# Attention with two feed-forward layers: the conversion steps of three weight blocks and four weight pieces at other turns of the attention loop

## The chip, the cores and the metric

One Trainium2 chip, one of its cores. The metric is device time in microseconds (us) of one execution, of which the median over the runs is taken; less is better. The engines are TensorE (PE, its weight loads PEld), VectorE (DVE), ScalarE (ACT), GpSimd (POOL) and SyncE (SP), which issues the DMAs here.

## What is computed

```python
# attention: q, k, v (2, 8, 768, 64); centroids (8, 16, 64)
q_assign = argmax(einsum('bhsd,hcd->bhsc', q_n, c_n)); k_assign likewise
mask = q_assign[:, :, :, None] == k_assign[:, :, None, :]
scores = where(mask, q @ k.T / sqrt(64), -1e9)
attn = softmax(scores)            # over keys
x = attn @ v                      # -> (1536, 512)
# first feed-forward layer: w_in (512, 2048), w_out (2048, 512), given as float64
x = (relu(x @ w_in) ** 2) @ w_out
# second: four experts, w1 (4, 512, 1024), w2 (4, 1024, 512)
out = sum_e p[:, e:e+1] * (relu(x @ w1[e]) @ w2[e])
```

## The kernel before

Every matrix product is made of several passes in fp32r: a tensor is split into a rounded part (`hi`) and what is left (`lo`).

**The attention loop.** There are 16 heads (batch times heads) of six query tiles of 128 rows, 96 tiles in all, and the loop `for g in range(NU)` makes one turn for each. Two heads form a pair, so a pair is 12 turns. Turn g does the following, on these engines:
- PE: the scores `s` of tile g+2 (L643), the transposes `t` of tile g in two halves (L676), a half of the product with the values (`po`, L690 and L692), and, in some turns, extra work in the two slots X1 and X2: transposes of the next pair's q and k (L388), its centroid scores (L469, turns 1 and 2 of a pair), their transposes (L485, turns 2 and 3) and those of the one-hot rows (L542, turn 7).
- DVE: the maximum `nb` of tile g+2 (L652) and the low halves `ptl` of tile g (L682), one behind each half's transposes; in some turns reductions of the assignment: `A` (L490, turns 2 and 3), `mx` (L526 in turn 4, L530 in turn 5).
- ACT: the exponential of tile g+1 (L663), the high halves `pth` (L681), and copies.
- POOL: the assignment's operations on `A` (L515 to L517 behind the first `mx`, L520 to L523 behind the second), splits of q, k and v, and the norm of the pair before.

The scores and the transposes have two PSUM buffers each. The transposes of tile g, half 0, use the buffer that `ptl` of tile g-1, half 0, has read; so they wait for that `ptl`, and the same holds for half 1.

**Order.** Within a turn the instructions are issued in an order written out by hand (`ORDER`, one list for even and one for odd turns; the engines run each its own part of it in order). DVE's part of an even turn is: M (the maximum of tile g+2), C, L0 and L1 (`ptl`), C, K, Y2; of an odd turn: M, C, L0, C, L1, Y2, K, C. C takes a queued step of the assignment, Y2 ends the work of slot X2 (its evacuation, `A` here), and K is the conversion slot: `convert()` issues what `convs` holds for this turn. R issues what `early` holds (loads, stacks, norm steps).

**Conversion.** The first layer's weights come as float64 words. `split64` (L145) makes a block of 512 columns into hi and lo in six steps: f1, f2, f4 (`tensor_scalar`, L161, L164, L167), f5, f6 (`scalar_tensor_tensor`, L172, L177), all on DVE on the one buffer `cva`, and f3, which is a cast on ACT (L182) and a subtraction on POOL (L186). There are four blocks of `w_in`'s first chunk, j = 0 to 3. Their steps are spread over the turns by `AT["conv"]` for j = 0, and for j = 1, 2, 3 over turns b0, b0+1, b0+2, b0+3, b0+4 and b0+9 with b0 = 30, 42, 54, which are turns 6 to 10 and 3 of a pair. The blocks are used at the end of the loop and behind it (`early_gemm1`).

**Pieces.** `load_piece` (L102) loads a quarter of half a chunk of the second matrix `w_out` (256 KB). Its eight DMAs go out in turns 46, 58, 70 and 82, two in each. They are converted behind the loop (`run_second`, `first_chunk`), the second half (pieces 4 to 7) by the third and fourth conversion there. Their buffer is that from which blocks 2 and 3 were read.

Of the kernel before, what the change touches and what calls it, by code (L numbers as in the profile page):

```python
# [26 lines left out]
WARM = [11, 3, 2, 6, 2, 3]  # L27
START = {'t': [0, 0, 1, 1], 'a': [3, 3, 4, 4, 7], 'stack1': 4, 'stack': 5, 'head': 2}
AT = {"stack1": (-11, -10), "stack": (-9, -9), "ohd": -7, "splitv": -3, "load": -10,
      "t": [-14, -13, -12, -11], "a": [-11, -10, -10, -9, -5], "conv": (8, 9, 10, 20, 21, 27), "pieces": 46,  # L30
      "norm": (11, 12, 16, 18, 19, 26), "in": (22, 34)}


# [1 line left out]
def moe_attention_kernel(  # L35
# [23 lines left out]
    NTT = S // 128  # L59
# [42 lines left out]
    def load_piece(half, n):  # L102

        if n == 0:
            raw_t[0, 1, half] = rawp.tile([128, 2048], F32, tag="raw", name="raw")
        r = raw_t[0, 1, half].bitcast(I32).rearrange("p (k f) -> p k f", k=2)
        kk, fs = n // 2, slice((n % 2) * 512, (n % 2) * 512 + 512)
        nc.sync.dma_start(out=r[:, kk, fs], in_=wo32[:, half * 2 + kk, fs])
# [36 lines left out]
    def split64(ci, part, j, cv, eng=None):  # L145

        jj = j % 2
        shp = [128, 512] if part else [128, 4, 128]

        def word(x):  # L150
            r = raw_t[ci, part, j // 2].bitcast(I32)
            if part == 0:
                r = r.rearrange("p (k f w) -> p k f w", k=4, w=2)
                return r[:, :, jj * 128:(jj + 1) * 128, x]
            return r.rearrange("p (k f w) -> p k f w", k=2, w=2)[:, jj, :, x]
        st = a_t[ci, part, j] = {}

        def f1():
            a = st["a"] = cv(shp)
            st["i"] = a.bitcast(I32)  # L160
            nc.vector.tensor_scalar(st["i"], word(1), 0x7FFFFFFF, None, op0=ALU.bitwise_and)  # L161

        def f2():
            nc.vector.tensor_scalar(st["a"], st["a"], 2.0 ** -15, None, op0=ALU.max)  # L164

        def f4():
            nc.vector.tensor_scalar(  # L167
                st["i"], st["i"], 3, 0x3FFFFFF8,
                op0=ALU.logical_shift_left, op1=ALU.bitwise_and)

        def f5():
            nc.vector.scalar_tensor_tensor(  # L172
                out=st["i"], in0=word(1), scalar=-0x40000000, in1=st["i"],
                op0=ALU.bitwise_and, op1=ALU.bitwise_or)

        def f6():
            nc.vector.scalar_tensor_tensor(  # L177
                out=st["i"], in0=word(0), scalar=29, in1=st["i"],
                op0=ALU.logical_shift_right, op1=ALU.bitwise_or)

        def f3h():
            nc.scalar.copy(w_block(part, j)[0], st["a"])  # L182

        def f3l():
            hi, lo = w_block(part, j)
            (eng or nc.gpsimd).tensor_tensor(lo, st["a"], hi.bitcast(F32), op=ALU.subtract)  # L186

        def f3():
            f3h()
            f3l()  # L190
        return [[f1, f2, f4, f5, f6], [f3], [f3h, f3l]]
# [20 lines left out]
    with tc.manual_schedule():  # L212
# [940 lines left out]
        def at(d, g, f):  # L1153
            d.setdefault(max(g, 0), []).append(f)
# [11 lines left out]
        for j in range(1, NH // 2):  # L1166
# [3 lines left out]
            for n, f in enumerate([pair_scores(j, 0), pair_scores(j, 1), pair_turn(j, 0),  # L1170
                                   pair_turn(j, 1), pair_hot(j)]):
                u = START["a"][n] if j == 1 else u0 + AT["a"][n]
# [8 lines left out]
        convs = {}  # L1181
        for j in range(NF):
            steps = [f for fs in split64(0, 0, j, cv_p[0])[0:2] for f in fs]
            b0 = (2 * j + 3) * NTT
            turns = AT["conv"] if j == 0 else [b0 + x for x in (0, 1, 2, 3, 4, 9)]
            for u, f in zip(turns, steps):
                at(convs, u, f)
        for n in range(8):
            at(convs, AT["pieces"] + n // 2 * 2 * NTT, lambda n=n: load_piece(n // 4, n % 4))
        for hp in range(NH // 2 - 1):  # L1190
            norm_steps(hp)

# [420 lines left out]
```

## Time and profile before

| | us |
|---|---|
| median of 3 runs | 1020.67 (1020.12 to 1021.22) |
| profiled execution | 1024.25 |
| its span, first to last instruction | 1022.5 |

| engine | busy us | share of the span |
|---|---|---|
| PE | 1007.5 | 99% |
| PEld | 895.3 | 88% |
| DVE | 730.6 | 71% |
| ACT | 556.3 | 54% |
| POOL | 611.9 | 60% |

The attention loop takes the stretch from about 19 to 252 us; the rest is the two layers. A row of groups reads: line, engine, operation, output<-inputs, shapes, count | busy us, mean ns of one | idle time of the engine before them, and what ended most of it. A row of a timeline reads: start, duration, engine, line, operation, count, and in brackets the idle time before it and who ended it. The first maximum that opens turn g is that of tile g+2.

### The profile page before, as it was taken

Reading aid. Unit: us, or ns where it says so; the run is one execution under the profiler, and the core shown is the slowest. Engines: PE = TensorE matmul, PEld = TensorE weight load, DVE = VectorE, ACT = ScalarE, POOL = GpSimd, SP = SyncE. Lnnn points to the kernel's source line nnn. Section 1 sums busy time; section 2 is a strip of 40 time slices with the busy share of each in tenths; the row PEclk is TensorE's granted clock in tenths of the full one; section 3 lists DMA queues with packets and bytes.
Section 4 is the critical chain, followed back from the end, with each engine's and each line's share of the span. In section 5 each row is a group of like instructions: output and inputs, shape, how many; then the busy total and the mean of one; then the engine's idle time right before and its main releaser. Section 6 shows DMA issues by size and latency. Waiting matters only on the chain.

```text
span 1022.5 us, 15046 instructions
## 1 busy us (share of the span) xinstructions
PE 1007.5 (99%) x5457; PEld 895.3 (88%) x5457; DVE 730.6 (71%) x1114; ACT 556.3 (54%) x1131; POOL 611.9 (60%) x630
## 2 busy tenths in 40 slices
PE   8999999999999999999999999999999999999998
PEld 7999999999888787888889889898888888898987
DVE  6889989888899987797586555567676555555554
ACT  5888888988655644456453443434443434433341
POOL 4577777773326654346586665766866756657550
PEclk8999999999999999999999999999999999999999
DMA  7468877853112212211012212222124122121101
GB/s 183 100 157 195 186 165 166 184 138 83 41 42 83 83 42 83 82 58 67 21 42 83 79 46 83 63 62 83 43 92 134 42 83 71 54 83 62 63 21 62
DMA packets 74067, 89.66 MB, mean 88 GB/s; under 512 B 27316, under 2 KB 50248, under 8 KB 73992
## 3 DMA queue, kind: packets, MB, share of 16 engines
q1 hardware_dynamic: 73992, 88.69, 31.8%
q8 instruction: 43, 0.70, 0.3%
q14 instruction: 32, 0.26, 0.1%
HBM read 62.58 MB, written 3.19 MB: 64 GB/s over the span
## 4 chain that ended last, share of the span: by engine, by line
PE 76%; DVE 18%; ACT 3%; issue 1%; POOL 1%; DMA 0%; DVEq 0%; POOLq 0%; ACTq 0%
PE bank L876 26%; PE bank L1038 26%; PE bank L904 7%; PE t L676 4%; PE s L643 4%; DVE ptl L682 3%; DVE nb L652 2%; PE po L690 2%; PE po L692 2%; PE bank L854 2%; DVE x L910 1%; PE m L469 1%; DVE cva L172 1%; DVE cva L167 1%; DVE cva L177 1%
## 5 line engine op out<-in xcount | busy, mean ns | idle before, releaser
L1048 DVE SCALAR_TENSOR_TENSOR x<-bank,pe_p,x 128x512 f32<-128x512 f32 x180 | 134.9, 750 | 182.8 <-PE bank L1038 182.7
L979 POOL TENSOR_TENSOR wxl<-raw,wxh 128x512 fp32r<-128x512 f32 x64 | 74.5, 1187 | 144.7 <-ACT wxh L978 144.7
L1038 PE MATMUL bank<-wzh,gb 128*128 128x512 f32 x384 | 135.4, 393 | 0.0
L1038 PE MATMUL bank<-wzh,ga 128*128 128x512 f32 x384 | 134.5, 393 | 0.0
L682 DVE TENSOR_TENSOR ptl<-t,pth 128x384 fp32r<-128x384 f32 x192 | 98.0, 549 | 18.0 <-ACT pth L681 17.4
L1007 ACT COPY fa<-bank 128x384 f32<-128x384 f32 x96 | 45.6, 475 | 117.8 <-PE bank L876 117.7
L876 PE MATMUL bank<-xa,wxh 128*128 128x384 f32 (+1 forms) x392 | 103.7, 345 | 0.0
L652 DVE TENSOR_REDUCE nb<-s 128x1 f32<-128x768 f32 x96 | 90.9, 946 | 11.5 <-PE s L643 10.8
L876 PE MATMUL bank<-xa,wyh 128*128 128x384 f32 (+1 forms) x344 | 89.3, 340 | 0.8 <-DVE fa L891 0.6
L663 ACT ACTIVATE p<-s,nb 128x768 f32<-128x768 f32 x96 | 88.0, 917 | 2.9 <-DVE nb L652 2.6
L681 ACT CAST pth<-t 128x384 fp32r<-128x384 f32 x192 | 84.0, 487 | 9.0 <-PE t L676 8.3
L676 PE MATMUL t<-identf,p 128*128 128x128 f32 x576 | 85.8, 276 | 1.6 <-DVE ptl L682 1.4
L643 PE MATMUL s<-k,q 80*128 80x384 f32 (+1 forms) x384 | 86.2, 346 | 0.0
L1038 PEld LDWEIGHTS bank<-wzh,ga 128*128 128x128 f32 x384 | 72.0, 188 | 12.3
L1038 PEld LDWEIGHTS bank<-wzh,gb 128*128 128x128 f32 x384 | 72.0, 188 | 12.2
L209 POOL TENSOR_TENSOR wyl<-raw,wyh 128x512 fp32r<-128x512 f32 x64 | 82.2, 1307 | 0.0
L992 POOL TENSOR_TENSOR wzl<-raw,wzh 128x1024 fp32r<-128x1024 f32 x31 | 74.8, 2412 | 10.0 <-ACT wzh L988 10.0
L690 PE MATMUL po<-pth,vv 128*128 128x256 f32 x288 | 80.4, 309 | 0.0
L876 PEld LDWEIGHTS bank<-xa,wxh 128*128 128x128 f32 x392 | 71.9, 188 | 7.6 <-ACT fa L1007 0.4
L904 PE MATMUL bank<-gb,wzh 128*128 128x512 f32 x240 | 78.0, 391 | 0.1
L676 PEld LDWEIGHTS t<-identf,p 128*128 128x128 f32 x576 | 67.0, 140 | 12.6 <-DVE ptl L682 9.7
L876 PE MATMUL bank<-rt,wyh 128*128 128x384 f32 (+1 forms) x264 | 72.3, 355 | 3.9 <-ACT fa L888 3.9
(279 smaller groups left out, 2613.1 us busy)
## 6 DMA issues: line engine op xcount, KB each, us to landing
raw<-in_moe_w_dram SPq DMA_DIRECT2D x64, 512.0 KB, 3.6
raw<-in_moe_w_in_dram SPq DMA_DIRECT2D x7, 1024.0 KB, 5.2
raw<-in_moe_w_out_dram SPq DMA_DIRECT2D x6, 1024.0 KB
k<-nkh SPq DMA_DIRECT2D x28, 192.0 KB, 3.4
q<-nqh SPq DMA_DIRECT2D x28, 192.0 KB, 4.5
nv<-in_v_dram SPq DMA_DIRECT2D x16, 192.0 KB, 3.9
out_dram<-x SPq DMA_DIRECT2D x12, 256.0 KB, 2.0
k<-nkl SPq DMA_DIRECT2D x14, 192.0 KB, 3.0
```

The lines of the kernel that those rows point to most:

```text
L209: eng.tensor_tensor(lo, a[m], hi.bitcast(F32), op=ALU.subtract)
L643: nc.tensor.matmul(s[:, j, 0:HALF], stk[i, nq][:, t * 128:(t + 1) * 128], stk[i, nk][:, j * HALF:(j + 1) * HALF], start=first, stop=not first)
L652: nc.vector.tensor_reduce(out=nb, in_=s_ps[u][:, :, 0:HALF], axis=AX.XY, op=ALU.max, negate=True)
L663: nc.scalar.activation(p, s_ps.pop(u)[:, :, 0:HALF], AF.Exp, bias=nb_t.pop(u), accum_out=sums_t[hp][:, i % 2, t:t + 1])
L676: nc.tensor.transpose(tp[:, j], p_sb[u][:, half, j * 128:(j + 1) * 128], identf)
L681: return (lambda: nc.scalar.copy(dh, tp), lambda: nc.vector.tensor_tensor(dl, tp, dh.bitcast(F32), op=ALU.subtract))
L682: lambda: nc.vector.tensor_tensor(dl, tp, dh.bitcast(F32), op=ALU.subtract))
L690: nc.tensor.matmul(po_t[pr], vt[i][:, kt], pth[:, kt], start=(kt == 0), stop=False)
L876: nc.tensor.matmul(ps, w[:, ks], x(xx)[:, kt], start=(first and kt == 0 and z == 0), stop=(kt == 1 and z == 2), skip_group_check=True)
L904: nc.tensor.matmul(o, a[:, d], b, start=(ft == 0 and z == 0), stop=(ft == 1 and z == 2))
L1038: nc.tensor.matmul(o, a, w[:, f], start=(f == 0 and z == 0), stop=(f == 1 and z == 2))
L1048: nc.vector.scalar_tensor_tensor(out=acc, in0=o, scalar=pc, in1=acc, op0=ALU.mult, op1=ALU.add)
```

## The change

The turns of all 24 conversion steps now stand in one table. Block 0 stays. Block 1 goes to turns 28, 28, 39, 39, 40, 42, block 2 to 51, 51, 52, 52, 63, 64, block 3 to 75, 75, 76, 76, 87, 89 (in the order f1, f2, f4, f5, f6, f3). Counted within a pair, these are turns 3 and 4 for all DVE steps. The pieces go out in turns 46, 58, 89 and 92.

```diff
-      "t": [-14, -13, -12, -11], "a": [-11, -10, -10, -9, -5], "conv": (8, 9, 10, 20, 21, 27), "pieces": 46,
+      "t": [-14, -13, -12, -11], "a": [-11, -10, -10, -9, -5], "conv": ((8, 9, 10, 20, 21, 27), (28, 28, 39, 39, 40, 42),
+               (51, 51, 52, 52, 63, 64), (75, 75, 76, 76, 87, 89)), "pieces": (46, 58, 89, 92),
...
         for j in range(NF):
             steps = [f for fs in split64(0, 0, j, cv_p[0])[0:2] for f in fs]
-            b0 = (2 * j + 3) * NTT
-            turns = AT["conv"] if j == 0 else [b0 + x for x in (0, 1, 2, 3, 4, 9)]
-            for u, f in zip(turns, steps):
+            for u, f in zip(AT["conv"][j], steps):
                 at(convs, u, f)
         for n in range(8):
-            at(convs, AT["pieces"] + n // 2 * 2 * NTT, lambda n=n: load_piece(n // 4, n % 4))
+            at(convs, AT["pieces"][n // 2], lambda n=n: load_piece(n // 4, n % 4))
```

## Rows read from the trace of the kernel before

**Rows 1.** The page, costliest groups: weight loads of the transposes.

```profile
L676 PEld LDWEIGHTS t<-identf,p 128*128 128x128 f32 x576 | 67.0, 140 | 12.6 <-DVE ptl L682 9.7
```

**Rows 2.** Chain of waits, 97 to 113 us (start, us on the chain, what).

```profile
99.62 0.34 DVE cva L161
...
101.75 0.77 DVE cva L164
...
104.34 1.02 DVE cva L167
...
109.58 0.60 DVE cva L177
```

**Rows 3.** Chain of waits, 173 to 203 us, shares by line.

```profile
by line: PE t L676 29.7%; PE s L643 28.5%; PE po L690 15.5%; PE po L692 15.1%; PE m L469 4.7%; PE m L388 4.4%; PE m L485 2.2%; PE m L542 0.7%; PE m L752 0.4%
```

**Rows 4.** Timeline of DVE, 174.8 to 190.2 us (turns 60 to 67).

```profile
177.96 0.96 DVE L652 TENSOR_REDUCE nb<-s 128x1 f32<-128x768 f32 x1 [0.81 <-PE s L643]
179.88 1.02 DVE L682 TENSOR_TENSOR ptl<-t,pth 128x384 fp32r<-128x384 f32 x2 [0.97 <-ACT pth L681]
...
183.08 0.55 DVE L490 TENSOR_REDUCE A<-m 128x192 f32<-128x384 f32 x1
...
184.41 0.54 DVE L526 TENSOR_REDUCE mx<-A 128x24 f32<-128x384 f32 x1
...
185.80 0.95 DVE L652 TENSOR_REDUCE nb<-s 128x1 f32<-128x768 f32 x1
...
188.94 1.01 DVE L682 TENSOR_TENSOR ptl<-t,pth 128x384 fp32r<-128x384 f32 x2
190.01 0.96 DVE L652 TENSOR_REDUCE nb<-s 128x1 f32<-128x768 f32 x1
```

**Rows 5.** Timeline of PEld, 183 to 191 us: transposes of turn 65.

```profile
185.47 0.31 PEld L676 LDWEIGHTS t<-identf,p 128*128 128x128 f32 x3 [0.28 <-DVE ptl L682]
...
185.93 0.31 PEld L676 LDWEIGHTS t<-identf,p 128*128 128x128 f32 x3 [0.15 <-DVE ptl L682]
```

**Rows 6.** Waits of PEld (us, times, longest): 96.7-113.6, 126.8-143.4, 157.1-173.8, 187.1-203.0.

```profile
PEld t L676 <- DVE ptl L682: 1.4, 4, 0.7
...
PEld t L676 <- DVE ptl L682: 1.0, 3, 0.7
...
PEld t L676 <- DVE ptl L682: 1.2, 4, 0.7
...
PEld t L676 <- DVE ptl L682: 0.3, 2, 0.2
```

**Rows 7.** Timeline of POOL, 184.5 to 187.7 us.

```profile
185.03 0.84 POOL L515 TENSOR_TENSOR A<-A,mx 128x384 f32<-128x384 f32 x1 [0.26 <-DVE mx L526]
185.96 0.52 POOL L516 TENSOR_SCALAR A<-A 128x384 f32<-128x384 f32 x1
```

**Rows 8.** Timelines of POOL and of DVE near 131 us (turn 43).

```profile
130.33 1.98 POOL L773 TENSOR_TENSOR xs<-xs,xm 128x384 f32<-128x384 f32 x2
...
131.75 0.85 DVE L164 TENSOR_SCALAR cva<-cva 128x512 f32<-128x512 f32 x1
```

**Rows 9.** Timelines of DVE, PEld and ACT in the last pair (turns 88 to 91).

```profile
239.57 1.02 DVE L682 TENSOR_TENSOR ptl<-t,pth 128x384 fp32r<-128x384 f32 x2
...
240.18 0.77 PEld L676 LDWEIGHTS t<-identf,p 128*128 128x128 f32 x6
...
242.00 0.37 ACT L708 COPY tmp<-po 64x256 f32<-64x256 f32 x1 [0.27 <-PE po L692]
...
243.79 1.02 DVE L682 TENSOR_TENSOR ptl<-t,pth 128x384 fp32r<-128x384 f32 x2
...
244.40 0.77 PEld L676 LDWEIGHTS t<-identf,p 128*128 128x128 f32 x6
```

**Rows 10.** Tile cva, last steps of a block (ns, min/median/max; start of first and last).

```profile
L182 ACT CAST wxh<-cva x10: 621/623/631, 92.4 to 454.4; 128x512 fp32r<-128x512 f32 x10
...
L186 POOL TENSOR_TENSOR wxl<-cva,wxh x4: 1288/1289/1289, 93.2 to 183.5; 128x512 fp32r<-128x512 f32 x4
```

**Rows 11.** Timelines of SP and DVE behind the loop; page, DMA issues (us to landing last).

```profile
236.79 1.18 SPq L764 DMA_DIRECT2D rb<-rd  x2
...
273.54 0.40 SPq L116 DMA_DIRECT2D raw<-in_moe_w_in_dram  x1
...
274.86 0.42 DVE L161 TENSOR_SCALAR cva<-raw 128x512 int32<-128x512 int32 x1
...
raw<-in_moe_w_in_dram SPq DMA_DIRECT2D x7, 1024.0 KB, 5.2
```

## The prediction, before the result was known

> **What bounds the kernel now.** I read the page first: TensorE (PE) is said to be busy 99% of the span, so something can only be won or lost where PE stands still, and the page's PE row hides short stops because ends of matmuls are modelled. The weight loads (PEld) show them: the loads for the transposes `t` waited 9.7 us in all for VectorE's (DVE's) `ptl` [rows 1]. So inside attention the question is where DVE makes PE wait, and the change moves DVE work there. I call one run of the loop over the 96 query tiles a turn, and number it within its pair of heads (turn 28 is turn 4 of its pair, 39 is turn 3).
>
> Second, the chain of waits in a stretch with a block's conversion (turns 30 to 36): it runs over DVE, and the conversion steps stand in it with 0.34 us (a step alone), 0.77 and 1.02 us (the same kind of step) and 0.60 us (a two-operand step) [rows 2]. These are net prices: what one step adds to DVE's row, overlap taken off. In a pair without such steps on DVE (from 173 us) the chain is PE alone [rows 3].
>
> Third, DVE's timeline in that pair. DVE stands idle 0.81 and 0.97 us before 177.96 and 179.88, in turns 1 and 2, where PE has pair scores to do besides. From 179.88 it runs without a gap to the end of the `ptl` pair of 188.94, at 189.95, and the idle time before the next maximum at 190.01 is only 0.06 us [rows 4]. Turn 3's conversion slot is behind the reduction `A` at 183.08, turn 4's just ahead of the maximum at 185.80: both in the gapless stretch, behind the idle time and not in it. And PE feels that stretch already: the transposes of turn 5 wait 0.28 and 0.15 us for `ptl` [rows 5].
>
> **What the change removes.** The five DVE steps of blocks 1, 2 and 3 leave turns 30 to 34, 42 to 46 and 54 to 58. The weight loads waited for `ptl` 1.4, 1.0 and 1.2 us in those three stretches, and 0.3 us in the same turns of a pair without conversion [rows 6]. So the three blocks cost PE 1.1 + 0.7 + 0.9 = 2.7 us now, though each brings over 3 us of DVE time: the rest falls into idle time that DVE has in turns 7 to 12. This 2.7 us is all there is to win: no other wait in the loop is due to these steps.
>
> **What it adds, by turn.** In the gapless stretch a step delays the next maximum, the next `ptl`, and through it the transposes of turn 5, which wait already; PE has no later idle time in which to catch up. So a step in turn 3 costs its net price in full. Behind it on DVE are queued that maximum, on which ScalarE's exponential waits, and `ptl`, on which PE waits. A step in turn 4 costs the same, less the little that DVE has left by 190.01; I take 0.1 off.
> - Turn 39: 0.34 + 0.60 = 0.94. Turns 51 and 75: 2 x 0.34 = 0.68 each. Turn 63: 0.60. Together 2.9 us.
> - Turn 4 slots uncontended: turn 28 0.58, turn 40 0.50, turns 52 and 76 0.84 each: 2.8 us. But the maximum `mx` of turn 4 (184.41 [rows 4]) releases GpSimd's (POOL's) three operations on `A`: the first starts at 185.03, 0.62 us behind `mx`, and runs 0.84 us, the second starts at 185.96 and runs 0.52 us [rows 7], so that the slot's first step falls on the end of the first and its second step on the second. What such a meeting does is seen at 131.75: a step took 0.85 us, and ended 0.29 us after POOL's operation did (130.33 + 1.98 = 132.31) [rows 8]; 1.02 against 0.34 us in rows 2 is the same. I add 0.4 us in turn 28, 0.1 in turn 40 (one step) and 0.5 each in turns 52 and 76, 1.5 us; the bounds are 0 and, with each step waiting out one POOL operation, about 3.
> - Turn 87, last pair, a 0.60 us step: the `ptl` pair of turn 88 ends at 240.59, and the second half of the loads that began at 240.18 starts at about 240.6 [rows 9], so there is no room either: 0.55 us (0 to 0.6).
> - The last steps of a block, a 0.62 us cast on ScalarE (ACT) and a 1.29 us subtraction on POOL [rows 10], move from turns 39, 51, 63 to 42, 64, 89. In 42 and 64 I cost them at nothing: in turns 6 to 8 DVE and ACT have gaps, and in turn 64 ACT would wait for the delayed maximum anyway; without that cover each costs up to 0.5 us. In turn 89 ACT has 0.27 us idle before the copy at 242.00, and the `ptl` pair of 243.79 ends at 244.81 when the second half of the loads from 244.40 is due [rows 9]: I take 0.5 us (0 to 0.6).
> - The four second-layer pieces of the last half move on SP's queue from turns 70 and 82 to 89 and 92. SP issues nothing between the row at 236.79 and the next weights at 273.54, and the first reader of these pieces is the conversion step at 274.86; weights take up to 5.2 us to land [rows 11], so the last ones, issued near 247, are there 20 us ahead. Nothing of PE waited for what they now stand ahead of. Zero, both ways.
>
> The rule that speaks most against the change is in the Trainium skill, "SBUF — State Buffer", section "Who interferes with whom": VectorE and GpSimd share one pair of SBUF ports under an exclusive lock, and whoever starts second waits for the whole instruction of the other. Rows 8 agree (0.85 us, ended just behind POOL's operation). By the rule the 1.5 us above stands; without it the sum would be 1.5 us smaller.
>
> Sum: 2.9 + 2.8 + 1.5 + 0.55 + 0.5 = 8.2 us added, 2.7 removed: 5.5 us longer. The profiled execution took 1024.25 us (span 1022.5 and 1.75 around it), so it would take 1029.8; the median of the runs is 3.6 us below the profiled one, and I carry the difference over: 1020.67 + 5.5 = **1026.2 us**.
>
> **Rivals.** (a) *The steps fit the idle time of the long turns.* If the 0.81 and 0.97 us [rows 4] could take them, all is won and nothing paid: 1020.67 - 2.7 = 1018.0, faster. For it: in a pair without conversion the chain is PE alone [rows 3], so DVE seems to have room. Against it: the idle time lies in turns 1 and 2, the slots behind it, and PE waits in turn 5 [rows 5]. It decides by whether the transposes of turn 5 wait longer than now. 7%. (b) *Most of turn 4 and of the last pair is hidden.* If a delay set in turn 4 is used up by gaps of turns 6 to 8, and the last pair has room, there remain turn 3's 2.9 us and some 0.8 us: 3.7 - 2.7 = 1.0 us, 1021.7, no difference. 11%. (c) *No collisions with POOL* in turn 4, the rest as forecast: 4.0 us, 1024.7. This is the forecast's own lower part, 25% by itself. (d) *The pieces come too late* and the second layer's conversion waits: it needs 20 us of lateness before the first microsecond is lost. Under 1%.
>
> **How the numbers follow.** Forecast with (c): 82%, of which 57% with the collisions. Its own span is from 1023.3 (no collision, the last pair half paid, 0.9 us less in turn 4) to 1028.2 (each turn-4 step waits out a POOL operation, 1.5 more, and a cast in turn 42 or 64 is not hidden, 0.5 more). With half of (b) taken in the range is 1022.0 to 1028.2. A measurement tells 0.2%, 2 us, from no change. Slower by more than that: 82%; within it: (b), 11%; faster: (a), 7%.
>
> **What would show it.** Right: in the profile after, loads of `t` wait for `ptl` in turns 5 (29, 41, 53, 65, 77) 0.7 to 2 us longer than the 0.43 of rows 5; the waits of turns 34, 46 and 58 are gone, so that those stretches show 0.3 us as the fourth of rows 6; the steps in turns 28, 52 and 76 last 0.6 us and more against 0.42 in turns 51 and 75. The total of that wait is some 5 us above the page's 9.7. Wrong: that total is below 9 us, or DVE has idle time between the steps and the next `ptl`. If pieces matter, DVE's steps of the second layer's third block wait for a DMA.

## The result, and the profile after

The changed kernel takes 1026.22 us (median of 6 runs), the kernel before 1021.14 us (6 runs): the ratio is 1.0053, with a 95% interval of 1.0036 to 1.0070, or 3.7 to 7.1 us. It is slower, by 5.1 us: clear of the interval, and 0.5% of the whole.

The two profiled executions differ by less, 1024.2 against 1022.5 us of span, and that has to be cleared up first. The busy time by stretch shows why (columns: stretch, its length, busy us of PE, PEld, DVE, ACT, POOL with the number of instructions, then PE's granted clock, DMA share, GB/s). The kernel before:

```profile
10.00:20.00 10.00, 8.64 (x52) 7.86 (x51) 5.40 (x14) 3.25 (x6) 6.16 (x8) 0.66 0.82 218
300.00:400.00 100.00, 95.40 (x410) 77.50 (x409) 90.87 (x121) 47.56 (x81) 50.54 (x42) 0.98 0.23 74
```

and the changed kernel:

```profile
10.00:20.00 10.00, 8.64 (x70) 7.77 (x69) 7.53 (x16) 5.14 (x10) 6.41 (x9) 1.00 0.88 223
300.00:400.00 100.00, 95.38 (x417) 77.47 (x416) 93.27 (x124) 48.60 (x83) 49.78 (x40) 1.00 0.21 66
```

In the profiled execution of before PE was granted 0.66 of its clock in the first stretch, and 0.57 from 387 to 391 us, which makes the 0.98 of the second:

```profile
387.00:391.00 4.00, 3.47 (x9) 2.77 (x10) 3.86 (x9) 0.98 (x2) 1.28 (x1) 0.57 0.48 196
```

Against the changed kernel it lost 2.7 us up to the loop's first turn and 1.5 us behind the loop by that. (Of the ten traces of this case three have such a fall behind the loop, and take 774.3 to 774.5 us from the end of turn 92 to the last instruction; the seven others take 772.9 to 773.0.) Between them, from the start of turn 0 to the end of turn 92, the loop is 233.00 us long and was 227.10: 5.9 us more. 5.9 - 2.7 - 1.5 = 1.7 is the difference of the spans. So the loop is compared, turn by turn.

The wait that the argument was about, on the page after and over the loop alone (18.8 to 250 us; us, times, longest); it answers to [rows 1]:

```profile
L677 PEld LDWEIGHTS t<-identf,p 128*128 128x128 f32 x576 | 66.7, 140 | 17.8 <-DVE ptl L683 14.8
```

```profile
PEld t L677 <- DVE ptl L683: 14.4, 46, 1.3
PEld m L470 <- POOL nql L398: 1.2, 3, 0.6
...
PEld po L691 <- DVE xs L710: 0.4, 1, 0.4
PEld s L644 <- ACT p L664: 0.2, 1, 0.2
```

The wait of the transposes for `ptl` grew from 9.7 to 14.8 us, 5.1 us. Two small waits are new: PE for `xs`, and PE for the exponential `p`. (Line numbers are one higher in the changed kernel.)

The length of a turn on PE, from the first score product of one turn to that of the next, gives the account. Turn 77 of before takes 2.39 us by it, and that of the changed kernel 3.20:

```profile
213.87 0.86 PE L643 MATMUL s<-k,q 128*128 128x384 f32 x4
...
216.26 0.88 PE L643 MATMUL s<-k,q 128*128 128x384 f32 x4
```

```profile
214.16 0.86 PE L644 MATMUL s<-k,q 128*128 128x384 f32 x4
...
217.36 0.86 PE L644 MATMUL s<-k,q 128*128 128x384 f32 x4
```

Only these turns differ by more than 0.04 us; "forecast" is the recorded price:

```
steps                      longer or shorter in turns      measured us  forecast
28 (f1, f2)                30 +0.69, 31 +0.18                  +0.87      +1.0
39 (f4, f5), 40 (f6)       41 +1.08, 42 +0.31, 43 +0.17        +1.56      +1.54
51 (f1, f2), 52 (f4, f5)   53 +0.79, 54 +0.97, 55 +0.19        +1.95      +2.02
63 (f6)                    65 +0.60                            +0.60      +0.60
75 (f1, f2), 76 (f4, f5)   77 +0.81, 78 +0.94, 79 +0.18        +1.93      +2.02
87 (f6)                    88 +0.45                            +0.45      +0.55
89 (cast, subtraction)     90 +0.15, 91 +0.37                  +0.52      +0.5
taken from 30-34           34 -0.59, 36 -0.29                  -0.88      -1.1
taken from 42-46           46 -0.59                            -0.59      -0.7
taken from 54-58           58 -0.61, 60 -0.17                  -0.78      -0.9
no step near               37 +0.23, 49 +0.07                  +0.30       0
```

The sum is 5.9 us. How a moved step lands is seen in turns 75 to 77 of the changed kernel. DVE's timeline (start, duration):

```profile
212.60 0.55 DVE L491 TENSOR_REDUCE A<-m 128x192 f32<-128x384 f32 x1
213.06 0.42 DVE L162 TENSOR_SCALAR cva<-raw 128x512 int32<-128x512 int32 x1
213.52 0.43 DVE L165 TENSOR_SCALAR cva<-cva 128x512 f32<-128x512 f32 x1
213.86 0.95 DVE L653 TENSOR_REDUCE nb<-s 128x1 f32<-128x768 f32 x1
214.73 0.55 DVE L527 TENSOR_REDUCE mx<-A 128x24 f32<-128x384 f32 x1
215.19 1.01 DVE L683 TENSOR_TENSOR ptl<-t,pth 128x384 fp32r<-128x384 f32 x2
216.11 0.42 DVE L168 TENSOR_SCALAR cva<-cva 128x512 int32<-128x512 int32 x1
216.57 0.87 DVE L173 SCALAR_TENSOR_TENSOR cva<-raw,cva 128x512 int32<-128x512 int32 x1
217.36 0.95 DVE L653 TENSOR_REDUCE nb<-s 128x1 f32<-128x768 f32 x1
```

and PEld's over the same turns:

```profile
215.79 0.31 PEld L677 LDWEIGHTS t<-identf,p 128*128 128x128 f32 x3 [1.08 <-DVE ptl L683]
216.25 0.31 PEld L677 LDWEIGHTS t<-identf,p 128*128 128x128 f32 x3 [0.16 <-DVE ptl L683]
...
218.83 0.31 PEld L677 LDWEIGHTS t<-identf,p 128*128 128x128 f32 x3 [0.92 <-DVE ptl L683]
```

DVE has no gap: f1 and f2 push the maximum, `mx` and `ptl` back by 0.80 us (213.06 to 213.86), and the transposes of turn 77 wait 1.08 us where those of turn 65 waited 0.28 in [rows 5]. f4 and f5, whose slot in turn 76 is behind that turn's `ptl`, do the same one turn later, to the transposes of turn 78 (0.92 us).

### The profile page after: what moved, and what is told of

It reads as the page before. It is cut to its first block, busy times and chain, and to the rows that moved or that the text cites. A ratio compares the mean times of both kernels' runs of the same rounds, so it can differ in the third digit from the quotient of the medians.

```text
span 1024.2 us, 15054 instructions
## 1 busy us (share of the span) xinstructions
PE 1005.3 (98%) x5457; PEld 891.1 (87%) x5457; DVE 728.9 (71%) x1114; ACT 557.9 (54%) x1131; POOL 610.9 (60%) x630
## 4 chain that ended last, share of the span: by engine, by line
PE 75%; DVE 16%; ACT 3%; POOL 2%; issue 2%; DMA 1%; SPq 1%; POOLq 0%; DVEq 0%; ACTq 0%
PE bank L1039 26%; PE bank L877 26%; PE bank L905 7%; PE t L677 4%; PE s L644 4%; PE po L691 2%; PE po L693 2%; DVE ptl L683 2%; PE bank L855 2%; DVE nb L653 1%; DVE x L911 1%; DVE cva L173 1%; DVE cva L178 1%; DMA k<-nkh 1%; PE m L470 1%
## 5 line engine op out<-in xcount | busy, mean ns | idle before, releaser
L677 PEld LDWEIGHTS t<-identf,p 128*128 128x128 f32 x576 | 66.7, 140 | 17.8 <-DVE ptl L683 14.8
L1039 PE MATMUL bank<-wzl,gb 128*128 128x512 f32 x192 | 75.8, 395 | 0.0
```

Source lines behind the costliest of these rows:

```text
L677: nc.tensor.transpose(tp[:, j], p_sb[u][:, half, j * 128:(j + 1) * 128], identf)
L1039: nc.tensor.matmul(o, a, w[:, f], start=(f == 0 and z == 0), stop=(f == 1 and z == 2))
```

## Experiments

**The pieces alone.** The kernel before with

```diff
-      ... "pieces": 46,
+      ... "pieces": (46, 58, 89, 92),
...
-            at(convs, AT["pieces"] + n // 2 * 2 * NTT, lambda n=n: load_piece(n // 4, n % 4))
+            at(convs, AT["pieces"][n // 2], lambda n=n: load_piece(n // 4, n % 4))
```

> The kernel before with the pieces alone moved (turns 46, 58, 89, 92); all conversion steps stay. My theory costs the pieces at nothing: no difference, within 1 us of 1021.1 us, and the loads of the transposes wait 9.7 us for the low halves as before. The rival, that the pieces carry part of the loss (landing late, or meeting other transfers in the last pair), would show 2 us or more above, and a wait for a DMA in the second layer's third conversion.

Measured: 1021.02 us against 1021.48 of before, ratio 0.9992 (0.9978 to 1.0005); the loop is 227.04 us (227.10), and the loads of the transposes wait 10.1 us for `ptl`. The pieces by themselves cost nothing that shows (0.5 us at most, by the interval). The loss is that of the steps.

**The old places by themselves.**

```diff
+            if j:
+                def last(f=steps[5], j=j):
+                    a_t[0, 0, j].update(a_t[0, 0, 0])
+                    f()
+                steps = [lambda: None] * 5 + [last]
             for u, f in zip(turns, steps):
                 at(convs, u, f)
```

> The kernel before without the five DVE steps of blocks 1, 2 and 3: these blocks are not converted, their last step works on what block 0 left. It prices the old places by themselves. My theory: 2.2 to 2.7 us less than before, 1018.4 to 1018.9 us, and the loads of the transposes wait 7 us for the low halves in place of 9.7. The rival: another wait behind it (POOL's split of the next pair, for which PE waits in turn 1 of two pairs) takes what is won, and the time stays near 1021.

Measured: 1019.63 us, ratio 0.9976 (0.9964 to 0.9989), 1.1 to 3.7 us less; the loop is 225.39 us, 1.7 less. (This kernel leaves the conversion of three blocks out: it prices the steps and is no version to use.) The waits of PEld over the loop:

```profile
PEld t L676 <- DVE ptl L682: 7.0, 34, 0.6
PEld m L388 <- ACT kqf L395: 1.0, 3, 0.5
PEld m L469 <- POOL nql L397: 0.9, 2, 0.6
PEld s L643 <- DMA k<-ohm: 0.5, 1, 0.5
```

The wait is 7.0 us as expected. The turns 34 to 36, 46 and 58 to 60 give 2.26 us (they are as short as in the changed kernel), the lower end of what was expected, and 0.5 us comes back, nearly all of it in turn 82 (+0.47), where PE waits for a DMA (the last row). The rival's wait, for POOL's `nql`, is 0.9 us as before. So the theory holds: 2.3 us is what the old places cost. That the wait of turn 82 comes of the gain is not shown: that turn is 0.2 to 0.3 us longer than before in three of the slower kernels below as well.

**All steps of a block in turn 3.** The changed kernel with this table, and the pieces as before:

```diff
+      ... "conv": ((8, 9, 10, 20, 21, 27), (39, 39, 39, 39, 39, 42), (51, 51, 51, 51, 51, 54), (63, 63, 63, 63, 63, 66)), "pieces": (46, 58, 70, 82),
```

> All five DVE steps of a block in turn 3 of a pair (39, 51, 63), the last step in turn 6, the pieces as before. My theory: from turn 3 a step costs PE its net price in full, and POOL is idle there, so no step is stretched: 3 x 0.34 + 2 x 0.60 = 2.2 us a block, all in the wait of turn 5 (41, 53, 65), which becomes 0.4 + 2.2 = 2.6 us; 6.7 us paid, 2.2 us won, some 4.5 us in all: 1025.6 us. The rival that the idle time of turns 1 and 2 takes steps of turn 3 gives 1019. The rival that steps meet POOL there as well gives over 3 us a block and 1028 us.

Measured: 1029.89 us, ratio 1.0086 (1.0061 to 1.0110), and 236.38 us for the loop: 9.3 us more, not 4.5. That the price is paid in full is confirmed: in turn 41 alone PE is 2.71 us later. Idle time takes nothing of it, and no step is stretched, so the rival that steps meet POOL there falls too, although its 1028 us lies nearer the measured time than the 1025.6 of the theory. But 2.71 is not 2.2, and turns 53, 54 (+3.65, +0.49) and 65, 66 (+3.20, +1.08) are longer still. The first has its reason on DVE's timeline, here in turn 51:

```profile
152.21 0.41 DVE L161 TENSOR_SCALAR cva<-raw 128x512 int32<-128x512 int32 x1
152.65 0.43 DVE L164 TENSOR_SCALAR cva<-cva 128x512 f32<-128x512 f32 x1
153.12 0.43 DVE L167 TENSOR_SCALAR cva<-cva 128x512 int32<-128x512 int32 x1
153.58 0.69 DVE L172 SCALAR_TENSOR_TENSOR cva<-raw,cva 128x512 int32<-128x512 int32 x1
154.31 0.69 DVE L177 SCALAR_TENSOR_TENSOR cva<-raw,cva 128x512 int32<-128x512 int32 x1
154.92 0.95 DVE L652 TENSOR_REDUCE nb<-s 128x1 f32<-128x768 f32 x1
```

Each step reads what the one before it wrote. From start to start f1, f2 and f4 take 0.44 to 0.47 us and f5 0.73, while f6, which has the unrelated maximum behind it, takes 0.61. My net prices of 0.34 and 0.60 were those of steps with a stranger behind them; a step whose successor needs it costs 0.1 us more. 152.21 to 154.92 is 2.71 us, which is turn 41's figure too. The second reason is in the busy time by stretch of the same run:

```profile
154.00:156.00 2.00, 0.16 (x1) 0.00 (x0) 1.97 (x4) 0.04 (x1) 0.00 (x0) 1.00 1.06 223
156.00:158.00 2.00, 1.16 (x7) 1.09 (x7) 2.00 (x4) 1.28 (x3) 1.43 (x3) 0.75 1.02 230
158.00:160.00 2.00, 2.00 (x11) 2.00 (x10) 1.69 (x4) 1.04 (x4) 1.02 (x2) 0.50 0.76 175
```

PE stood for 3.0 us, and then ran at half its clock (0.50) from 157.0 to 160.4 us. In turn 65 it was the same; in turn 41, after a stop as long, it was not. The 1.4 and 1.6 us beyond 2.71 go with the clock.

**The slot of turn 4 ahead of POOL's operations.** The changed kernel with

```diff
-            for a in ORDER[par]:
+            order = list(ORDER[par])
+            if g % 12 == 4 and not par:
+                order.remove("K")
+                order.insert(order.index("C"), "K")
+            for a in order:
```

> The changed kernel with the conversion slot of turn 4 (28, 40, 52, 76) put ahead of the step that starts POOL's three operations, and so ahead of both low halves. Nothing else moves. If meetings with POOL stretch the steps (in the changed kernel 0.87 and 0.92 us for a 0.68 us step in turns 76 and 52, 0.62 for a 0.43 us step in turn 28), they are 0.68 and 0.43 us here, and turns 53 to 55 and 77 to 79 are longer than before by 1.9 us less the stretch (0.2) plus the 0.1 that a step behind the low halves had hidden: 1.85 us. If my first size of these meetings (0.5 us a turn) was right, they are 1.5 us longer. If the steps' lengths do not change, POOL is not what stretched them.

Measured, one run: 1028.21 us (before 1021.33, one run beside it, as in the three experiments that follow). The steps of turn 76 are 0.42 and 0.69 us (DVE's timeline):

```profile
216.71 0.42 DVE L168 TENSOR_SCALAR cva<-cva 128x512 int32<-128x512 int32 x1
217.16 0.69 DVE L173 SCALAR_TENSOR_TENSOR cva<-raw,cva 128x512 int32<-128x512 int32 x1
217.77 0.55 DVE L527 TENSOR_REDUCE mx<-A 128x24 f32<-128x384 f32 x1
```

where the changed kernel had 0.87 us for the second (in turn 52 as well; the 0.92 us in the expectation is a step of block 0), with these operations of POOL beside it:

```profile
215.35 0.84 POOL L516 TENSOR_TENSOR A<-A,mx 128x384 f32<-128x384 f32 x1 [3.98 <-DVE mx L527]
216.28 0.63 POOL L517 TENSOR_SCALAR A<-A 128x384 f32<-128x384 f32 x1
216.99 1.32 POOL L518 TENSOR_TENSOR A<-A,wgt 128x384 f32<-128x384 f32 x1
```

Turns 53 and 77 are 1.86 us longer than before each, and no turn behind them: 1.85 was expected with a stretch of 0.2 us, 1.5 with my first size. So meetings with POOL are real, and cost 0.2 us a turn, not 0.5. Elsewhere this kernel lost on new ground: in turn 28 the slot now stands ahead of `ptl` and f1 waits 0.31 us for POOL's last step of block 0, whose buffer it needs (turn 29 +1.20); in turn 64 block 2's subtraction stands ahead of POOL's three operations, so that the second `mx` waits 0.49 us for them (turn 67 +0.47); and turns 41 and 42 are 3.24 us longer, with the clock at 0.50 from 126 to 128 us after a stop of 1.95 us.

**Two terms of the last pair.** The changed kernel with block 3's last entry at 94 in place of 89:

> The changed kernel with block 3's last step (the cast on ACT, the subtraction on POOL) in turn 94 in place of 89, just ahead of a stretch in which ACT waits 2.9 us for PE. My theory: the cast in front of the exponential is what makes turns 90 and 91 longer by 0.15 and 0.37 us; both are gone, and nothing comes in their place: 0.5 us less than the changed kernel in these turns. The rival, that these turns are longer through the two pieces loaded there, leaves them as they are.

Measured, one run: 1025.34 us. Turns 90 and 91 are as before, within 0.04 us; the 0.52 us is the cast's, and the pieces have no part in it.

The changed kernel with f6 of block 3 at 86 in place of 87:

> The changed kernel with block 3's last DVE step in turn 86 in place of 87. In turn 87 it stands ahead of the addition to xs that frees the one accumulator of the value product, and PE waits 0.4 us for that addition in turn 88. In turn 86 no such addition follows. Theory now: turn 88's 0.45 us is gone and at most 0.35 us comes back in turns 87 and 88 as a wait of the transposes for the low halves. Rival (the recorded working): the step costs 0.55 us by the low halves wherever it stands in the last pair.

Measured, one run: 1025.35 us. The wait for `xs` (0.4 us above) is gone, and turn 88 is 0.27 us longer than before in place of 0.45, by the transposes' wait:

```profile
PEld t L677 <- DVE ptl L683: 0.3, 2, 0.2
```

(stretch 234 to 245 us). In turn 87 the price was paid through the accumulator, not through `ptl`.

**Two turns earlier, into the long turns of the trace.** The changed kernel with

```diff
+      ... "conv": ((8, 9, 10, 20, 21, 22), (26, 26, 37, 37, 38, 42),
+               (49, 49, 50, 50, 61, 64), (73, 73, 74, 74, 85, 89)), "pieces": (46, 58, 89, 92),
```

> The changed kernel with every DVE step two turns earlier: turns 1 and 2 of a pair (26, 37, 38, 49, 50, 61, 73, 74, 85), the two that are longest in the trace; block 0's last step in turn 22 to make room. Theory: what stands in turn 1 is ahead of DVE's idle 0.81 and 0.97 us and is hidden (turns 37, 49, 61, 73: nothing paid, but POOL is busy there, so steps may last up to 1 us longer and POOL's split for the pair scores may come later by as much); what stands in turn 2 is behind it and costs its full price in turns 3 to 5 (26: 0.8; 38: 0.6; 50 and 74: 1.2 to 1.5). In all 4 us paid against 7.9 in the changed kernel. Rival (the long turns take all): turns 26 to 29, 50 to 53 and 74 to 77 are as long as before. Rival (place does not matter): as the changed kernel.

Measured, one run: 1025.40 us. The loop is 231.50 us, 4.4 more than before (5.9 in the changed kernel). What stands in turn 1 is free: turns 49, 61 and 73 differ by 0.05 us or less, and 37 by the 0.24 that the changed kernel has as well, though the steps last longer there, as DVE's timeline for turn 73 shows in its first two rows:

```profile
204.89 0.87 DVE L162 TENSOR_SCALAR cva<-raw 128x512 int32<-128x512 int32 x1
205.79 1.12 DVE L165 TENSOR_SCALAR cva<-cva 128x512 f32<-128x512 f32 x1
...
208.65 0.49 DVE L168 TENSOR_SCALAR cva<-cva 128x512 int32<-128x512 int32 x1
209.17 1.39 DVE L173 SCALAR_TENSOR_TENSOR cva<-raw,cva 128x512 int32<-128x512 int32 x1
```

POOL's operations beside those first two rows are

```profile
204.46 1.02 POOL L398 TENSOR_TENSOR nql<-kqf,nqh 128x384 fp32r<-128x384 f32 x1
205.43 1.19 POOL L728 TENSOR_TENSOR rb<-rb,xs 128x384 f32<-128x384 f32 x1
```

What stands in turn 2 costs more than in turn 4: turns 27 to 29 +1.30, 40 and 41 +0.68, 51 to 53 +1.82, 75 to 77 +1.84; 5.6 us where I had put 4. The steps there meet POOL (1.39 us for 0.69), and the slot stands ahead of the evacuation `A`, for which PE waits now (2.6 us in three turns). Both rivals fall: of the two long turns one hides steps, the other does not.

**The steps in DVE's idle time.** The changed kernel with this table, and the pieces as before:

```diff
+      ... "conv": ((8, 9, 10, 20, 21, 27), (30, 33, 33, 34, 37, 39), (42, 45, 45, 46, 49, 51), (54, 57, 57, 58, 61, 63)), "pieces": (46, 58, 70, 82),
```

> The steps where DVE stands idle: of each block one in turn 6 (30, 42, 54), two in turn 9, one in turn 10, the fifth in turn 1 of the next pair (37, 49, 61), ahead of the idle 0.81 and 0.97 us; the last step in turn 3 and the pieces as before. My theory: nearly all is hidden, 0.1 us a block at most is left, so it comes within 0.5 us of the kernel without steps: 1018.5 to 1019.5 us, faster than both. The rival that DVE's order and POOL's port make such steps cost as much wherever they stand gives 1021 or more, with the waits of turns 10 and 12 moved to turns 0 to 3.

Measured: 1019.58 us, ratio 0.9982 (0.9969 to 0.9995): 0.5 to 3.2 us faster than before, 6.6 us below the changed kernel, and level with the kernel without steps (1019.63). In the loop it is 1.1 us below before and 7.0 below the changed kernel; what the medians differ by beyond that goes with the granted clock, which was 1.00 over the whole of seven of these twelve runs and of four of the 29 of before. PEld's waits:

```profile
PEld t L676 <- DVE ptl L682: 7.0, 34, 0.6
PEld m L469 <- POOL nql L397: 1.9, 5, 0.7
...
```

The wait for `ptl` is that of the kernel without steps to the tenth, so all three blocks' steps are hidden. What is left of their price, 0.6 us of the loop (226.01 against 225.39), is PE's wait for POOL's `nql` in turns 37, 38, 49 and 50 (0.7 us more), less 0.2 us of turn 82's wait; f6 now stands beside that operation, and how much of the 0.7 us is due to it these runs do not say. This is the version that beats both.

## Why the prediction was right, and where its terms were not

- **What bounds it.** The prediction has this right. DVE is the engine that PE waits for in turn 5, and it runs there without a gap behind the idle time of turns 1 and 2. The wait grew by 5.1 us, where "some 5 us" was written. Rival (a), that the idle time takes the steps, would need turn 5 unchanged; it is 0.60 to 1.08 us longer in turns 41, 53, 65 and 77.
- **Where turn 4's price lands.** One turn later than the prediction's signs said. The slot of turn 4 is behind that turn's `ptl`, for which the transposes of turn 5 wait, and ahead of turn 5's, for which those of turn 6 wait. So turn 29 is as before (+0.01), though f1 and f2 stand in turn 28, and the price is in turns 30, 42, 54 and 78. For the same reason the waits of turns 34, 46 and 58 are gone, as was said, but their stretches do not come down to 0.3 us: they show 1.3, 0.9 and 1.6 us in the changed kernel (1.4, 1.0 and 1.2 in [rows 6]). The sum is not touched by it.
- **Turn 3 at the full net price.** The mechanism is right (turn 65: 0.60 for 0.60), the size of a pair of dependent steps was not: 0.79 to 0.81 us in turns 53 and 77 for a forecast 0.68. The term that was mis-sized is the price of a step, 0.34 us, read off the chain in [rows 2] where another's instruction follows; with its own successor behind it it is 0.46.
- **Meetings with POOL.** Right in kind, too large: 0.2 us in turns 28, 52 and 76 and none in turn 40, 0.6 us for 1.5. I let each of two steps wait for an operation; in the trace f4 starts as POOL's first operation ends, takes its turn ahead of the second (which then lasts 0.63 in place of 0.52 us), and only f5 waits, to 0.53 us behind the end of that second operation. The sign named for these meetings, steps of 0.6 us and more, came for the second step alone (0.62 us in turn 28, 0.87 in 52 and in 76); the first stayed at 0.42. The missing 0.12 us a pair in the line above, six pairs in all with those of f4 and f5, is 0.7 us the other way: the two errors hid each other, and each row of the table that adds time came out within 0.15 us. That part of the agreement is luck.
- **What is won.** 2.26 us in place of 2.7: the difference of the waits in [rows 6] overstates what the turns lose, as the wait of 0.71 us in turn 34 of before goes with a turn longer by 0.59. The length of the turn is the better measure.
- **Other waits.** The 0.3 us in turns 37 and 49, PE's wait for POOL's `nql`, is no term of the change: turn 37 is 0.23 us longer in the changed kernel and as before with f6 at 86, which is the same kernel up to there, and in the kernel with the pieces alone turn 48 is 0.38 us longer than before and turn 49 0.45 us shorter. It comes and goes between executions.
- **The last pair.** The sum is right (0.97 us for 1.05), the path of one half is not: f6 in turn 87 delays the addition that frees the accumulator; of the low halves' path only 0.27 us would have been paid from turn 86.
- **Pieces.** Nothing, as forecast. In the changed kernel the first reader starts at 278.06 us without waiting.

The profiled execution was put at 1029.8 us, the profiled time plus the sum; it took 1025.99, because the one of before had lost 4.2 us to the clock. The medians are touched less, but not by nothing: of the 29 runs of before in the experiments the four with a mean granted clock of 1.00 took 1019.9 to 1020.5 us and the sixteen with 0.998 took 1020.6 to 1022.5, while four of the changed kernel's six had 1.00. So the 5.9 us of the loop says better than the medians' 5.1 us what the change costs, and that the median of 1026.22 us meets the forecast 1026.2 to the tenth is luck.

What stays open: why the clock fell after three of six stops of 1.95 to 3.0 us and not after the others, and whether f6 can be placed so that `nql` waits less; the latter was not tried, as 0.6 us is less than these runs tell apart.

## What to carry to other kernels

Before work is moved into a turn because the turn is long, see on the engine's own timeline whether the slot is ahead of the idle time or behind it: here two turns made the difference between free and full price. Price such a step from start to start, and take 0.1 us more where its own successor follows at once. And price the old places by a run without the work: 2.3 us of turns were won there, of which the whole kept 1.7, for another wait took 0.5 back.

## What the runs showed of the hardware

- A DVE conversion step of 128x512 that lasts 0.42 us takes 0.34 us from its start to that of the next when an unrelated instruction follows and 0.46 when the follower reads its result; one of two operands, 0.69 us, takes 0.60 or 0.73.
- Two DVE conversion steps that met POOL lasted 0.87 and 1.12 us in place of 0.42, one of two operands 1.39 in place of 0.69; an operation of POOL that met a step was drawn out in turn, from 0.52 to 0.63 us. The first two ended 0.28 and 0.29 us behind the POOL operation that ran when they began (205.48 and 206.62 us). The Trainium skill, "SBUF — State Buffer", section "Who interferes with whom", says that of VectorE and GpSimd whoever gets the shared port pair first keeps it for its whole instruction, and the other blocks; these ends agree.
- PE's granted clock was 0.50, the 1.2 GHz level, in a stretch behind stops of 3.0, 3.0 and 1.95 us, and stayed at 1.00 behind stops of 3.0, 2.1 and 2.1 us. Where it fell, the turns came out 1.4 to 1.6 us longer than what the steps had added on DVE (2.71, 2.71 and 1.66 us).
